# Two MLPs behind a hashed attention: who converts the late weights, and how many conversion steps stand between the second layer's banks

## The chip, the cores and the metric

The kernel runs on one core of one Trainium2 chip. The metric is device time in microseconds (us) of one execution. TensorE (PE) multiplies matrices; its weight loads (PEld) run beside the products. VectorE (DVE), ScalarE (ACT) and GpSimd (POOL) work on tiles, and SyncE (SP) issues DMAs. Each engine takes its instructions in the order in which they were written, and waits on semaphores for the others.

## The reference

Attention with a hash mask, then two MLPs on the same 1536 tokens of width 512. The change lies in the first MLP and in what it prepares for the second.

```
x = attention(q, k, v, proj)                   # 1536 x 512
g = x @ w_gate; val = x @ w_val                # 512 -> 1536
y = (g * sigmoid(g) * val) @ w_out             # 1536 -> 512
h = y @ w_in                                   # 512 -> 1024
solu = h * softmax(h); ln = normalised(solu) * g_ln
out = ln @ w_out2                              # 1024 -> 512
```

The weights are float64 in memory. Every product is made of three, high by high, high by low and low by high, of float32r parts, so every weight is turned from float64 to float32 on the chip and then split into a high part and a low part (the rest).

## The kernel before, in words

**Groups.** The hidden width 1536 is 12 slices of 128, taken in six groups t = 0 to 5 of two slices. The tokens are three blocks of 512. For each group come six *units* (two slices by three blocks, function `hidden`, L1103): a unit is 24 products of 128x512, twelve for the gate and then twelve for the value, in two PSUM banks, and there are two banks of each kind. ScalarE applies Silu to the gate bank into `sg` (L1110), VectorE multiplies it by the value bank (L1111), ScalarE rounds the result to `ah` (L1113), VectorE takes the rest `al` (L1116). Then comes the *second layer* of the group (`summed`, L1127 to L1129): for each of the three blocks four banks `y` of six products each, twelve banks in all. Four PSUM banks serve them, so bank k + 4 cannot begin before bank k has been read. In group 0 ScalarE copies each bank to `yf` (L1137), in the later groups VectorE adds it to `yf` (L1139).

**Conversions.** Beside this runs a generator `stream` of 25 *pieces* of weights, each a 1 MB DMA into a buffer `raw` (two of them, L944 to L952), and conversion in *steps*, each of which is one call of `go(stream)`. `to_float32` is six VectorE instructions (L47, L51, L53, L57, L62, L64) from `raw` to the one buffer `wf`; L64 stands in a step with the ScalarE copy that follows it. Then ScalarE takes the high part (L1039) and VectorE the low part (L958). A piece of kind 1 (first layer) or 2 (second layer) is seven steps. The *late* pieces are for the second MLP: kind 3 are four row blocks of `w_in`, from which sums of blocks are made as well (`blocks3`; GpSimd makes t2, t3 and t4 at L989 to L1002), and kind 4 are four pairs of row blocks of `w_out2`, scaled by `g_ln`, split in place in `raw` and stored to DRAM (`parked`, L1025). Pieces 3/0 and 3/2 are last in group 0, 3/1 in group 1, 3/3 in group 2, 4/0 in group 3, 4/2 in group 4, 4/4 and 4/6 in group 5. The buffer `raw` of piece n is fetched again, for piece n + 2, when piece n has done with it.

**Order.** The order on every engine is that of the Python code (`manual_schedule`). A unit takes one step behind its products and up to three more, ending at the step "copied". In the second layer steps stand ahead of the reading of each bank: in group 0 two per bank (24 over three blocks), in groups 1 to 4 one, two, one, two (18 over three blocks). A step that comes when the next piece may not yet begin (`reached`) does nothing.

Of the kernel before, what the change touches and what calls it, by code (L numbers as in the profile page):

```python
# [9 lines left out]
F32 = mybir.dt.float32  # L10
# [6 lines left out]
ALU = mybir.AluOpType  # L17
# [11 lines left out]
def run(steps):  # L29
    for _ in steps:  # L30
        pass
# [6 lines left out]
def to_float32(nc, raw, f):  # L38

    words = raw.bitcast(I32).rearrange("p (n t) -> p n t", t=2)
    low, high = words[:, :, 0], words[:, :, 1]
    bits = f.bitcast(I32)


    nc.vector.tensor_scalar(  # L47
        bits, high, 1, 1, ALU.logical_shift_left, ALU.logical_shift_right
    )
    yield  # L50
    nc.vector.tensor_scalar_max(f, f, FLOOR)  # L51
    yield
    nc.vector.tensor_scalar(  # L53
        bits, bits, 3, 0x3FFFFFF8, ALU.logical_shift_left, ALU.bitwise_and
    )
    yield
    nc.vector.scalar_tensor_tensor(  # L57
        bits, high, -0x40000000, bits, ALU.bitwise_and, ALU.bitwise_or
    )
    yield  # L60

    nc.vector.tensor_scalar_mul(high, low.bitcast(U32), 2.0 ** -29)  # L62
    yield
    nc.vector.tensor_tensor(bits, bits, high, ALU.add)  # L64
# [3 lines left out]
def hash_attention_then_two_mlps(  # L68
# [16 lines left out]
    nc = tc.nc  # L85
# [12 lines left out]
    BLK = 512  # L98
# [68 lines left out]
    for g in range(4):  # L167
        m = (g + 1) % 2
# [8 lines left out]
    up, down, both = slice(0, D), slice(D, P), slice(0, P)  # L177
# [41 lines left out]
    with at:  # L219
# [13 lines left out]
        one = sm.tile([P, 1], F32, tag="one", name="one", bufs=1)  # L233
# [4 lines left out]
        raw, turned, bits_of, last_of = {}, {}, {}, {}  # L238
# [475 lines left out]
        def go(work):  # L714

            next(work, None)
# [157 lines left out]
    gl = sm2.tile([P, KF2], F32, name="gl", bufs=1)  # L874
# [16 lines left out]
    def halves(pool):  # L891
        return [
            pool.tile([P, 2, DM], R32, tag=tag, name=tag) for tag in ("hi1", "lo1")
        ]
# [4 lines left out]
    with ExitStack() as m1:  # L899
# [16 lines left out]
        def weights1(f):  # L916
            hi, lo = halves(ws)
            w1_of[f] = [x.rearrange("p n (k f) -> p n k f", k=KD) for x in (hi, lo)]
            return hi, lo

        hi, lo = weights1(0)
# [35 lines left out]
        def low(dst, src, hi):  # L957
            nc.vector.tensor_sub(dst, src, hi.bitcast(F32))  # L958

        def blocks3(n, wf):  # L960

            i, d = divmod(n, KH)
            left, right, other = wf[:, :BLK], wf[:, BLK:], w1f[d]
            b11, b21, b22, t1, t2, t3, t4 = (
                [w3_of[x][:, m, d] for m in range(2)]
                for x in ("b11", "b21", "b22", "t1", "t2", "t3", "t4")
            )
            if i == 0:  # L970
                nc.scalar.copy(b11[0], left)
                nc.scalar.copy(other, right)
                yield "copied"
                low(b11[1], left, b11[0])
                nc.vector.tensor_sub(left, right, left)
                nc.scalar.copy(t1[0], left)
                yield "copied"
                low(t1[1], left, t1[0])
                return
            nc.scalar.copy(b21[0], left)  # L980
            nc.scalar.copy(b22[0], right)  # L981
            yield "copied"
            low(b21[1], left, b21[0])
            low(b22[1], right, b22[0])
            add, sub = nc.gpsimd.tensor_add, nc.gpsimd.tensor_sub
            for block, first, t in ((b22, sub, t3), (b11, add, t2), (b21, sub, t4)):
                hi, lo = (x.bitcast(F32) for x in block)
                if first is sub:
                    sub(other, hi, other)  # L989
                else:  # L990
                    add(other, other, hi)
                add(other, other, lo)
                rounded(*t, other)

        def rounded(hi, lo, src):

            n = src.shape[1:]
            one = unit1
            for _ in n[1:]:
                one = one.unsqueeze(2)  # L1000
            nc.gpsimd.tensor_mul(hi, src, one.to_broadcast(list(src.shape)))
            nc.gpsimd.tensor_sub(lo, src, hi.bitcast(F32))  # L1002

        def convert(piece, raw):
            kind, n = piece[2:4]
            wf = wr.tile([P, 2 * DM], F32, tag="wf", name="wf", bufs=1)
            yield from to_float32(nc, raw, wf)
            if kind == "4":

                hi, lo = (  # L1010
                    raw.bitcast(R32)[:, m * 2 * DM:(m + 1) * 2 * DM].rearrange(
                        "p (m e) -> p m e", m=2
                    ) for m in range(2)
                )
                wf = wf.rearrange("p (m e) -> p m e", m=2)
                for m in range(2):
                    nc.scalar.mul(hi[:, m], wf[:, m], gl[:, n + m:n + m + 1])
                yield "copied"
                for m in range(2):
                    nc.vector.scalar_tensor_tensor(  # L1020
                        lo[:, m], wf[:, m], gl[:, n + m:n + m + 1], hi[:, m].bitcast(F32),
                        ALU.mult, ALU.subtract,
                    )
                for m, x in enumerate((hi, lo)):
                    nc.sync.dma_start(parked[m][n // 4][:, n % 4:n % 4 + 2], x.bitcast(F32))  # L1025
                return
            if kind == "3":
                yield from blocks3(n, wf)
                return
            if kind == "1":  # L1030
                hi, lo = weights1(n)
            else:
                hi, lo = [
                    w2.tile([P, 2, DM], R32, tag=f"{x}2", name=f"{x}2") for x in ("hi", "lo")
                ]
                for m in range(2):
                    w2_of[n + m] = [x[:, m] for x in (hi, lo)]
            hi, lo = (x.rearrange("p m e -> p (m e)") for x in (hi, lo))
            nc.scalar.copy(hi, wf)  # L1039
            yield "copied"  # L1040
            low(lo, wf, hi)

        def conversions():

            raws = [fetch(piece) for piece in pieces[:AHEAD]]
            for n, piece in enumerate(pieces):
                while piece[:2] > reached:
                    yield
                yield from convert(piece, raws[n])
                if n + AHEAD < len(pieces):  # L1050
                    raws.append(fetch(pieces[n + AHEAD]))
                yield
# [100 lines left out]
        stream = conversions()  # L1153
# [3 lines left out]
        for t in range(TH):  # L1157
            for unit in range((FT + 1) * NBLK):
                f, blk = divmod(unit, NBLK)
                reached = (t, unit)  # L1160
                if t == TH - 1 and unit == FT * NBLK:

                    yh = xpool.tile([P, KD, NT], R32, tag="h", name="yh")
                    yl = xpool.tile([P, KD, NT], R32, tag="l", name="yl")
                    run(stream)
                    for n in (0, 2):
                        parts = halves(ws)
                        for x, stored in zip(parts, parked):
                            nc.sync.dma_start(x.bitcast(F32), stored[0][:, n:n + 2])
                        for m in range(2):  # L1170
                            w4_of[n + m] = [x[:, m] for x in parts]
                    nc.scalar.activation(half, half, AF.Exp)
                work = hidden(t * FT + f, blk) if f < FT else summed(t, blk)
                go(work)
                if f < FT:

                    go(stream)
                    go(before)
                    for _ in range(3):
                        if next(stream, None) == "copied":  # L1180
                            break
                    go(work)
                    before = work
                    continue

                go(before)
                before = lows(blk - 1) if t == TH - 1 and blk else iter(())
                for d in range(KD):
                    if blk and t == TH - 1:
                        go(before)  # L1190
                    else:
                        go(stream)
                        if t == 0 or d % 2:
                            go(stream)
                    go(work)
        sums_of(1)
# [264 lines left out]
```

## Time and profile before

| | |
|---|---|
| median of three runs | 718.27 us (717.79 to 718.29) |
| the profiled execution | 717.94 us, its span 716.2 us |
| PE busy | 688.2 us, 96% of the span |
| DVE busy | 588.0 us, 82% |
| ACT busy | 353.4 us, 49% |
| POOL busy | 255.2 us, 36% |
| mean granted TensorE clock | 0.988 of full speed |

The span runs from the first to the last instruction; 1.74 us lie around it. The profile puts each idle time of an engine down to the instruction that ended it. A matmul is pipelined, so its duration is longer than the pitch from start to start, and the pitch is what counts.

### The profile page before, as it was taken

How to read it: one execution, taken by the hardware profiler on the slowest of the kernel's cores; microseconds unless marked ns; L12 is line 12 of the kernel's file. 1: busy time of each engine (PE TensorE's matmuls, PEld its weight loads, DVE VectorE, ACT ScalarE, POOL GpSimd, SP SyncE). 2: the span in 40 equal slices, each digit the busy share in tenths (PEclk: the TensorE clock that was granted, in tenths of full speed). 3: DMA queues.
4: the chain of work that ended last, by engine and by line, in shares of the span. 5: the costliest groups of instructions: out<-in, count | busy, mean ns of one | idle time of the engine just before them, and what ended most of it. 6: DMA issues, size and time to landing. Idle time of an engine off the chain costs nothing.

```text
span 716.2 us, 10379 instructions
## 1 busy us (share of the span) xinstructions
PE 688.2 (96%) x3653; PEld 585.4 (82%) x3653; DVE 588.0 (82%) x1046; ACT 353.4 (49%) x724; POOL 255.2 (36%) x271
## 2 busy tenths in 40 slices
PE   8999999999999999879989889999999999999998
PEld 6999999999998888658768668778778887888877
DVE  8989999999999988897866896785887887756771
ACT  7898898988989742324122112213113534424332
POOL 6656556655534510370000370000000177775300
PEclk9999999999999999989999999999999999999999
DMA  5684563654514122313122111331333530222211
GB/s 176 168 206 119 157 164 86 159 153 104 145 44 146 18 88 91 117 59 117 59 72 95 69 59 59 118 118 60 118 117 119 176 118 1 88 89 89 89 45 45
DMA packets 39492, 73.72 MB, mean 103 GB/s; under 512 B 5352, under 2 KB 26920, under 8 KB 38672
## 3 DMA queue, kind: packets, MB, share of 16 engines
q1 hardware_dynamic: 39440, 73.06, 33.4%
q8 instruction: 29, 0.48, 0.3%
q14 instruction: 23, 0.19, 0.1%
HBM read 40.90 MB, written 7.34 MB: 67 GB/s over the span
## 4 chain that ended last, share of the span: by engine, by line
PE 72%; DVE 21%; ACT 4%; issue 2%; DMA 1%; SPq 0%; DVEq 0%; ACTq 0%
PE h L1103 21%; PE s L539 9%; PE t L589 8%; PE h L1216 7%; PE av L624 4%; PE av L628 3%; PE o L1331 3%; PE o L1329 3%; PE o L1330 3%; DVE wf L57 2%; DVE wf L64 2%; PE pp L498 2%; DVE yf L1139 2%; PE pp L455 2%; DVE raw L62 1%
## 5 line engine op out<-in xcount | busy, mean ns | idle before, releaser
L1103 PE MATMUL h<-xh,hi 128*128 128x512 f32 x288 | 113.9, 396 | 4.5 <-DVE sg L1111 4.5
L1103 PE MATMUL h<-xl,hi 128*128 128x512 f32 x288 | 113.5, 394 | 0.0
L1103 PE MATMUL h<-xh,lo 128*128 128x512 f32 x288 | 112.5, 394 | 0.0
L602 DVE TENSOR_TENSOR el<-t,eh 128x384 fp32r<-128x384 f32 x192 | 97.7, 550 | 9.7 <-ACT eh L598 8.7
L574 ACT ACTIVATE e<-s,nm 128x768 f32<-128x768 f32 x96 | 97.7, 1017 | 4.6 <-DVE nm L559 4.0
L598 ACT CAST eh<-t 128x384 fp32r<-128x384 f32 x192 | 83.9, 492 | 18.5 <-PE t L589 16.8
L550 DVE TENSOR_REDUCE top<-s 128x1 f32<-128x768 f32 x96 | 90.6, 944 | 0.7 <-PE s L539 0.5
L589 PE MATMUL t<-idr,e 128*128 128x128 f32 x576 | 80.1, 274 | 0.5 <-DVE el L602 0.3
L589 PEld LDWEIGHTS t<-idr,e 128*128 128x128 f32 x576 | 67.9, 140 | 9.4 <-DVE el L602 3.9
L1127 PE MATMUL y<-ah,hi 128*128 128x512 f32 x144 | 59.7, 415 | 15.2 <-DVE yf L1139 13.2
L1103 PEld LDWEIGHTS h<-xh,hi 128*128 128x128 f32 x288 | 55.1, 191 | 16.5 <-DVE sg L1111 4.9
L1111 DVE TENSOR_TENSOR sg<-h,sg 128x512 f32<-128x512 f32 x36 | 24.9, 691 | 48.5 <-PE h L1103 39.7
L1103 PEld LDWEIGHTS h<-xl,hi 128*128 128x128 f32 x288 | 55.0, 191 | 11.4
L1103 PEld LDWEIGHTS h<-xh,lo 128*128 128x128 f32 x288 | 54.8, 191 | 11.5
L624 PE MATMUL av<-eh,vs 128*128 128x384 f32 x186 | 64.0, 344 | 0.0
L1113 ACT CAST ah<-sg 128x512 fp32r<-128x512 f32 x36 | 22.4, 623 | 81.4 <-DVE sg L1111 81.4
L1129 PE MATMUL y<-ah,lo 128*128 128x512 f32 x144 | 57.8, 402 | 0.0
L1128 PE MATMUL y<-al,hi 128*128 128x512 f32 x144 | 57.8, 401 | 0.0
L539 PE MATMUL s<-ka,qa 128*128 128x384 f32 x192 | 54.6, 365 | 1.5 <-ACT e L574 1.4
L1066 POOL TENSOR_TENSOR sf<-yh 128x256 f32<-128x256 f32 x5 | 3.7, 736 | 142.1 <-ACT yh L1142 142.1
L1039 ACT CAST hi<-wf 128x1024 fp32r<-128x1024 f32 x17 | 17.8, 1048 | 72.6 <-DVE wf L64 72.6
L989 POOL TENSOR_TENSOR w1f<-w3b,w1f 128x512 f32<-128x512 f32 x4 | 7.0, 1760 | 129.7 <-ACT w3b L981 129.5
(274 smaller groups left out, 1609.0 us busy)
## 6 DMA issues: line engine op xcount, KB each, us to landing
raw<-in_moe_w_out_dram SPq DMA_DIRECT2D x10, 1024.0 KB
raw<-in_moe_w_gate_dram SPq DMA_DIRECT2D x12, 512.0 KB
raw<-in_moe_w_val_dram SPq DMA_DIRECT2D x12, 512.0 KB
ka<-kt SPq DMA_DIRECT2D x30, 192.0 KB
moved<-u SPq DMA_DIRECT2D x9, 512.0 KB
raw<-in_moe_w_in_dram SPq DMA_DIRECT2D x4, 1024.0 KB
parked<-raw SPq DMA_DIRECT2D x8, 512.0 KB
v<-in_v_dram SPq DMA_DIRECT2D x8, 384.0 KB
```

The source lines that it names most:

```text
L539: nc.tensor.matmul(s[:, n, :HALF], a[:, rows], m[:, n * HALF:(n + 1) * HALF], start=first, stop=not first,)
L550: nc.vector.tensor_reduce(top[:, 1:2], s_of[i][:, :, :HALF], AX.XY, ALU.max, negate=True)
L574: nc.scalar.activation(e, s_of.pop(i)[:, :, :HALF], AF.Exp, bias=nm[:, 1:2], scale=nm[:, 0:1], accum_out=total_of[p, n][:, j, c:c + 1],)
L589: nc.tensor.transpose(t[:, m, :], e_of[i][:, g, m * P:(m + 1) * P], idf)
L598: nc.scalar.copy(half_tile(eh_of, i, g), t_of[i, g])
L602: last_of[i] = nc.vector.tensor_sub(half_tile(el_of, i, g), t_of.pop((i, g)), half_tile(eh_of, i, g).bitcast(F32),)
L624: nc.tensor.matmul(av, vj[:, c], eh_of[h][:, c, :], start=c == 0, stop=c == C - 1)
L1103: nc.tensor.matmul(ps[n], a[:, n, kk, :], x[:, kk, blk * BLK:(blk + 1) * BLK], start=kk == 0 and a is hi and x is xh, stop=kk == KD - 1 an ...
L1127: nc.tensor.matmul(p, hi[:, cols], ah, start=f == t * FT, stop=False)
L1128: nc.tensor.matmul(p, hi[:, cols], al, start=False, stop=False)
L1129: nc.tensor.matmul(p, lo[:, cols], ah, start=False, stop=f == (t + 1) * FT - 1)
L1216: nc.tensor.matmul(dst, a[m](d), w3_of[b][:, l, d], start=start and n == 0, stop=n == 3 * KH - 1, skip_group_check=True,)
```

## The change

Late pieces: of kind 3 with i = 0 (3/0 and 3/1), VectorE keeps the low part of b11; the difference for t1 and its split go to GpSimd, in `raw` as scratch. With i = 1 (3/2, 3/3) the low part of b22 goes to GpSimd. In kind 4 ScalarE writes the scaled weights where the low part will stand, then copies the high part, and GpSimd subtracts. So no step holds more than one VectorE instruction. In the second layer three steps stand to four banks (one, none, one, one) in groups 1 to 4, and five (one, two, one, one) in group 0.

```diff
@@ blocks3
-        def blocks3(n, wf):
+        def blocks3(n, wf, raw):
...
+            add, sub = nc.gpsimd.tensor_add, nc.gpsimd.tensor_sub
             if i == 0:
                 nc.scalar.copy(b11[0], left)
                 nc.scalar.copy(other, right)
                 yield "copied"
                 low(b11[1], left, b11[0])
-                nc.vector.tensor_sub(left, right, left)
-                nc.scalar.copy(t1[0], left)
-                yield "copied"
-                low(t1[1], left, t1[0])
+                one = raw.bitcast(F32)[:, :BLK]
+                sub(one, other, b11[0].bitcast(F32))
+                sub(one, one, b11[1].bitcast(F32))
+                rounded(*t1, one)
                 return
...
             low(b21[1], left, b21[0])
-            low(b22[1], right, b22[0])
-            add, sub = nc.gpsimd.tensor_add, nc.gpsimd.tensor_sub
+            sub(b22[1], right, b22[0].bitcast(F32))
@@ convert, kind 4
+                both = lo.bitcast(F32)
                 for m in range(2):
-                    nc.scalar.mul(hi[:, m], wf[:, m], gl[:, n + m:n + m + 1])
+                    nc.scalar.mul(both[:, m], wf[:, m], gl[:, n + m:n + m + 1])
                 yield "copied"
-                for m in range(2):
-                    nc.vector.scalar_tensor_tensor(
-                        lo[:, m], wf[:, m], gl[:, n + m:n + m + 1], hi[:, m].bitcast(F32),
-                        ALU.mult, ALU.subtract,
-                    )
+                nc.scalar.copy(hi, both)
+                nc.gpsimd.tensor_sub(lo, both, hi.bitcast(F32))
@@ the second layer's banks
-                        go(stream)
-                        if t == 0 or d % 2:
+                        if t == 0 or d != 1:
+                            go(stream)
+                        if t == 0 and d == 1:
                             go(stream)
                     go(work)
```

**VectorE, second layer of group 3, before** (`yf` is a bank's addition; the other rows are conversions, L1020 the low part of piece 4/0):

```order
L57 SCALAR_TENSOR_TENSOR wf<-raw,wf 128x1024
L1139 TENSOR_TENSOR yf<-y,yf 128x512
L62 TENSOR_SCALAR raw<-raw 128x1024
L64 ISA wf<-raw,wf 128x2048
L1139 TENSOR_TENSOR yf<-y,yf 128x512
L1020 SCALAR_TENSOR_TENSOR raw<-wf,gl,raw 128x512 x2
L1139 TENSOR_TENSOR yf<-y,yf 128x512
L47 TENSOR_SCALAR wf<-raw 128x1024
L51 TENSOR_SCALAR wf<-wf 128x1024
L1139 TENSOR_TENSOR yf<-y,yf 128x512
L53 TENSOR_SCALAR wf<-wf 128x1024
L1139 TENSOR_TENSOR yf<-y,yf 128x512
```

The same place now (the addition is L1137 in the changed file):

```order
L57 SCALAR_TENSOR_TENSOR wf<-raw,wf 128x1024
L1137 TENSOR_TENSOR yf<-y,yf 128x512 x2
L62 TENSOR_SCALAR raw<-raw 128x1024
L1137 TENSOR_TENSOR yf<-y,yf 128x512
L64 ISA wf<-raw,wf 128x2048
L1137 TENSOR_TENSOR yf<-y,yf 128x512 x3
L47 TENSOR_SCALAR wf<-raw 128x1024
L1137 TENSOR_TENSOR yf<-y,yf 128x512
L51 TENSOR_SCALAR wf<-wf 128x1024
L1137 TENSOR_TENSOR yf<-y,yf 128x512
```

Five additions had eight conversions between and ahead of them; now eight additions have five.

**VectorE, from the second `w_in` piece of group 0 to the first `sg` of group 1, before** (`lo` is a kind 1 weight's low part, `sg` the product of the first unit):

```order
L47 TENSOR_SCALAR wf<-raw 128x1024
L51 TENSOR_SCALAR wf<-wf 128x1024
L53 TENSOR_SCALAR wf<-wf 128x1024
L57 SCALAR_TENSOR_TENSOR wf<-raw,wf 128x1024
L62 TENSOR_SCALAR raw<-raw 128x1024
L64 ISA wf<-raw,wf 128x2048
L958 TENSOR_TENSOR lo_4379<-wf,hi_4378 128x1024
L47 TENSOR_SCALAR wf<-raw 128x1024
L51 TENSOR_SCALAR wf<-wf 128x1024
L53 TENSOR_SCALAR wf<-wf 128x1024
L57 SCALAR_TENSOR_TENSOR wf<-raw,wf 128x1024
L1111 TENSOR_TENSOR sg<-h_4390,sg 128x512
```

The same place now:

```order
L47 TENSOR_SCALAR wf<-raw 128x1024
L51 TENSOR_SCALAR wf<-wf 128x1024
L53 TENSOR_SCALAR wf<-wf 128x1024
L57 SCALAR_TENSOR_TENSOR wf<-raw,wf 128x1024
L62 TENSOR_SCALAR raw<-raw 128x1024
L64 ISA wf<-raw,wf 128x2048
L1109 TENSOR_TENSOR sg<-h_4382,sg 128x512
L958 TENSOR_TENSOR lo_4410<-wf,hi_4409 128x1024
```

The first `sg` moves ahead of five conversions, which follow it.

**ScalarE, second layer of group 0, before** (`yf` are the banks' copies, `w3b` and `w3t` parts of the late pieces):

```order
L1137 COPY yf<-y 128x512
L971 CAST w3b_3963<-wf 128x512
L972 COPY w1f_96<-wf 128x512
L976 CAST w3t_3966<-wf 128x512
L1137 COPY yf<-y 128x512 x4
L980 CAST w3b_3964<-wf 128x512
L981 CAST w3b_3965<-wf 128x512
L1137 COPY yf<-y 128x512 x3
L1039 CAST hi_4378<-wf 128x1024
L1137 COPY yf<-y 128x512 x4
L1110 ACTIVATE sg<-h_4389 128x512
```

The same place now:

```order
L1135 COPY yf<-y 128x512
L972 CAST w3b_3963<-wf 128x512
L973 COPY w1f_96<-wf 128x512
L1135 COPY yf<-y 128x512 x6
L981 CAST w3b_3964<-wf 128x512
L982 CAST w3b_3965<-wf 128x512
L1135 COPY yf<-y 128x512 x5
L1037 CAST hi_4409<-wf 128x1024
L1108 ACTIVATE sg<-h_4381 128x512
```

The `w3t` copy is gone, the second piece's two copies stand behind the seventh bank and not the fifth, and the last five banks come ahead of the kind 1 copy.

## Rows read from the trace of the kernel before

**Rows 1.** Longest waits of PE, 280 to 590 us: total, times, longest.

```profile
PE y L1127 <- DVE yf L1139: 13.2, 15, 2.3
PE h L1103 <- DVE sg L1111: 4.5, 1, 4.5
PE y L1127 <- ACT yf L1137: 1.8, 1, 1.8
```

**Rows 2.** Windows: stretch, length, busy PE, PEld, DVE, ACT, POOL, PEclk, DMA, GB/s.

```profile
281.96:341.85 59.89, 53.63 (x218) 42.99 (x216) 50.69 (x51) 18.90 (x32) 19.71 (x12) 0.91 0.26 88
341.85:397.42 55.57, 51.85 (x217) 41.44 (x216) 40.59 (x54) 12.02 (x18) 0.00 (x0) 0.97 0.23 76
397.42:454.80 57.38, 52.01 (x218) 41.07 (x217) 45.88 (x53) 11.41 (x17) 19.05 (x12) 0.97 0.22 74
454.80:507.47 52.67, 50.53 (x218) 40.19 (x216) 39.89 (x53) 11.60 (x17) 0.00 (x0) 1.00 0.29 100
507.47:560.13 52.66, 50.53 (x217) 40.19 (x216) 42.96 (x57) 12.12 (x19) 0.00 (x0) 1.00 0.28 100
```

**Rows 3.** The chain in order of time, six units of group 4: start, us, what.

```profile
474.97 32.67 PE h L1103 x144
```

**Rows 4.** Timeline of PE, groups 0 and 1: start, us, instruction, [idle before, releaser].

```profile
290.72 0.57 PE L1127 MATMUL y<-ah,hi 128*128 128x512 f32 x1 [1.80 <-ACT yf L1137]
302.26 0.39 PE L1103 MATMUL h<-xh,hi 128*128 128x512 f32 x1
320.52 0.80 PE L1103 MATMUL h<-xh,hi 128*128 128x512 f32 x1 [4.46 <-DVE sg L1111]
```

**Rows 5.** Windows behind two PE waits, columns as above; PEclk is third from the end.

```profile
290.90:294.20 3.30, 3.30 (x9) 2.54 (x10) 3.16 (x5) 1.22 (x3) 0.00 (x0) 0.52 0.29 101
318.20:324.90 6.70, 4.38 (x10) 3.48 (x11) 5.01 (x6) 2.16 (x3) 0.58 (x1) 0.51 0.09 20
```

**Rows 6.** Timeline of DVE, second layer of group 3, GpSimd idle.

```profile
457.05 1.22 DVE L57 SCALAR_TENSOR_TENSOR wf<-raw,wf 128x1024 int32<-128x1024 int32 x1
458.19 0.68 DVE L1139 TENSOR_TENSOR yf<-y,yf 128x512 f32<-128x512 f32 x1
458.79 0.69 DVE L62 TENSOR_SCALAR raw<-raw 128x1024 int32<-128x1024 uint32 x1
459.51 1.23 DVE L64 CUSTOM_DVE_ANT_0 wf<-raw,wf 128x2048 uint16<-128x2048 uint16 x1
461.53 1.42 DVE L1020 SCALAR_TENSOR_TENSOR raw<-wf,gl,raw 128x512 fp32r<-128x512 f32 x2 [0.19 <-ACT raw L1017]
```

**Rows 7.** Timeline of DVE beside a busy GpSimd, groups 0 and 2.

```profile
303.34 2.19 DVE L57 SCALAR_TENSOR_TENSOR wf<-raw,wf 128x1024 int32<-128x1024 int32 x1
305.56 1.67 DVE L62 TENSOR_SCALAR raw<-raw 128x1024 int32<-128x1024 uint32 x1
409.79 0.68 DVE L1139 TENSOR_TENSOR yf<-y,yf 128x512 f32<-128x512 f32 x1
```

**Rows 8.** Timeline of POOL, first and last of the twelve instructions of piece 3/3.

```profile
404.61 1.29 POOL L989 TENSOR_TENSOR w1f<-w3b,w1f 128x512 f32<-128x512 f32 x1 [85.83 <-ACT w3b L981]
423.52 1.61 POOL L1002 TENSOR_TENSOR w3t<-w1f,w3t 128x512 fp32r<-128x512 f32 x1
```

**Rows 9.** Timeline of DVE and ACT, group 0: late conversion, bank copies, first `sg` of group 1.

```profile
287.46 0.62 ACT L971 CAST w3b<-wf 128x512 fp32r<-128x512 f32 x1 [3.31 <-DVE wf L64]
290.08 2.04 ACT L1137 COPY yf<-y 128x512 f32<-128x512 f32 x4
309.49 1.05 ACT L1039 CAST hi<-wf 128x1024 fp32r<-128x1024 f32 x1 [10.53 <-DVE wf L64]
319.79 0.68 DVE L1111 TENSOR_TENSOR sg<-h,sg 128x512 f32<-128x512 f32 x1
```

**Rows 10.** Timeline of SP and a window of the DMAs: a weight fetch and its end.

```profile
296.36 0.37 SPq L952 DMA_DIRECT2D raw<-in_moe_w_out_dram  x1
...
300.00:302.00 2.00, 2.00 (x10) 1.69 (x9) 1.93 (x3) 0.00 (x0) 1.92 (x2) 1.00 0.29 119
```

More of the change, by code (lines that the diff above doesn't have):

```diff
@@ L1027, in convert @@
             if kind == "3":
-                yield from blocks3(n, wf)
+                yield from blocks3(n, wf, raw)
                 return
```

## Prediction

> **What bounds the kernel now.** I read the waits of PE first, from 280 to 590 us, where the diff works [rows 1]. PE waits there for almost one thing: the additions of the second layer's banks to `yf`, 13.2 us in 15 waits, with 1.8 us for a ScalarE copy and 4.5 us for one late `sg`. Then I cut the stretch at the first product of each second layer, into five stages (0 to 4, one second layer and the next group's six units each), and asked for the busy times of each [rows 2]. They last 59.89, 55.57, 57.38, 52.67 and 52.66 us. The chain of waits gives what a stage needs: 144 products in 32.67 us, 0.227 us each [rows 3]. A stage has 72 + 144 = 216 products, so 49.0 us. The rest is loss: 10.9, 6.6, 8.4, 3.7 and 3.7, together 33.3 us. That is more than the 19.5 us of waits. A stall costs PE part of its overlap besides (groups 3 and 4 lose 3.7 us each), and behind the longer waits the granted clock is 0.51 to 0.52, the 1.2 GHz level, for 3.3 or 6.7 us [rows 5].
>
> VectorE is not full: it is busy 39.9 to 50.7 us of each stage [rows 2]. It is late where the work is bunched. Twelve banks of 6 x 0.227 = 1.36 us come in 16.3 us, and between them stand 18 conversion steps. The bank k + 4 waits for bank k's addition, so the eighth addition is the last one that PE can wait for, and it must be done 11 x 1.36 = 15.0 us into the second layer.
>
> **The change part by part.** I count from a stage's first product. Alone, a conversion instruction comes every 0.69 to 0.73 us (L47, L51, L53, L62) or 1.22 to 1.26 us (L57, L64), an addition every 0.60 [rows 6]. Beside a busy GpSimd the first kind takes 1.67 and the second 2.2, about 1.0 us more each, while an addition stays at 0.68 [rows 7].
>
> *Steps, groups 3 and 4.* L57 starts at 2.25 [457.05 against 454.80, rows 2, 6]. Now: L57 to 3.4, two additions to 4.6, L62 to 5.3, an addition to 5.9, L64 to 7.1, three additions (the sixth bank ends at 8.2) to 9.1, L47 to 9.8, the seventh to 10.4, L51, the eighth. L51 may meet the new GpSimd instruction: ScalarE's scaling ends at about 8.6, its new 128x1024 copy (1.05 as in [rows 9]) at 9.7, and GpSimd then takes, by twice the 1.29 of a 128x512 one, an estimated 2.6 us [rows 8]. If L51 waits for all of it, the eighth addition is done at 13.6. PE wants it at 15.0. No stall; a gain of 3.7 in each. Two VectorE instructions of 0.71 [rows 6] go, and the estimated 2.6 us on GpSimd stands beside PE work.
>
> *Steps, group 1.* GpSimd now has four instructions for 3/1, from 8.3 (L64 ends at 7.1, two ScalarE copies follow) to about 15. L47 and L51 become 1.67. Additions: fourth 7.7, fifth 9.1 behind L958, sixth 9.7, seventh 12.0, eighth 14.3. Slack 0.7; gain 6.6.
>
> *Steps, group 2.* GpSimd runs thirteen instructions instead of twelve, which took 404.61 to 425.13, 1.71 each [rows 8], so from 8.3 to about 30. The eighth addition is done at 14.3 as in group 1. Behind it everything is slow: L53 15.7, two additions, L57 19, L62 and two additions, L64 at about 23, ScalarE's copy 24, L958 26, L47 and L51, then the first `sg` at 29.6. PE wants it when the third unit reaches its value bank, 16.3 + 2.5 x 5.45 = 29.9. The second `sg` comes at 35.5 and is wanted at 35.4. I take 0.5 us of loss: gain 7.9.
>
> *Group 0.* Before: ScalarE's second copy stood behind `w3t`, so PE resumed at 290.72 [rows 4]; at 1.36 us per bank it would have been 288.8. Now that copy comes behind `w1f`, at about 289.1: 0.4 us of loss. But 3/0 now has four GpSimd instructions from 288.6 on, beside the six conversions of 3/2. Alone these would end at 294.2, with 3.6 us for the four about 297.8. The eighth bank's copy now stands behind the two copies that wait for that: done at 299.5, wanted at 297.4. So a new stall of 2.1, and perhaps the low clock behind it. The units start at 300.9 (302.5 with the low clock) against 302.26 [rows 4]. Thirteen GpSimd instructions follow, to 320. L958, the wait for GpSimd to read `wf`, and six conversions at 1.4 to 2.2 us put L64 at 310.3; ScalarE's copy and Silu to 312.0, first `sg` to 312.7. It was wanted two and a half units after the start: 314.5 or 316. Before, it was done at 320.5 [rows 9] and cost 4.46 us and a low clock [rows 4]. The second `sg` (L958 2.2, `al`, L47, L51, L53 first) is done at 321.1, wanted at 320.0 or 321.6. Two and a half units more end at 334.7 or 335.2. I take 335.0 against 341.85: gain 6.9.
>
> *Costs taken at nothing.* Steps moved into the units of groups 1 to 5: the units there issue the same sequence as before from the second `sg` on (in group 1 from the fifth), and of the 49.0 us VectorE has 9 free in stage 3 and 6 in stage 4 [rows 2]; without that cover a late `sg` costs what stage 0 paid. The buffer `raw` of 3/0 and 3/1 is held until GpSimd has done, some 7.5 us, and with it a fetch on SP's queue. A fetch lands about 4.3 us after its issue (issued at 296.36, the last DMA time about 300.6) [rows 10]: in group 0 at 299.3, wanted at 300.3; in group 1 at 19, wanted at 24. In kind 4 the store waits for GpSimd until about 12.3 instead of 8.2 and holds the next fetch behind it on SP; that lands at about 20, wanted at 24. If one of these fetches is late, VectorE's queue stands, with additions or `sg` behind it; each us would be a us.
>
> Sum: 6.9 + 6.6 + 7.9 + 3.7 + 3.7 = 28.8. From the profiled execution's 717.94 (span 716.2 and 1.74 around it) that leaves 689.1; I say 689. The median before lies 0.33 above that execution. Bounds: all the loss goes, 717.94 - 33.3 = 684.6; or GpSimd makes it worse, below.
>
> What a VectorE instruction loses to GpSimd is 1.0 us here, the rest of the GpSimd instruction in progress [rows 7, 8]. The Trainium skill (SBUF — State Buffer, "SBUF: two separate sides") speaks against giving GpSimd work: the shared port pair is "an exclusive lock, not a bandwidth split", held for the whole instruction, for VectorE instructions that read two SBUF inputs or use both ports. The trace agrees: conversions go from 0.69 to 1.67, the additions, one input of which is PSUM, stay. By that rule the 128x1024 instruction blocks L51 for its whole length, which is the upper case taken above; by 1.0 us the eighth addition would be done at 12.2 and the sum is the same.
>
> **The rivals.** *GpSimd's longer work keeps VectorE late.* If each extra GpSimd instruction costs VectorE all of its 1.65 us and not 1.0, the late conversions of group 0 end 2.6 us later and its first `sg` and second `sg` some 7 us later in all: stage 0 gains nothing. In stage 2 the `sg` come 4 us late: gain 4. Groups 1, 3 and 4 keep 6.6 + 3.7 + 3.7. Sum 18, so 700. For it: group 0 lost 10.9 us beside twelve such instructions. Against: groups 3 and 4, which lost 7.4 with GpSimd idle, are mended by the order alone.
>
> *The waits move from `yf` to `sg` (the other side).* Nine steps per stage leave the second layer and stand in the units. If the first `sg` is late past the third unit's value bank in every stage as it was in group 0, each pays 4.46 of wait [rows 4] and half of 6.7 us at the low clock [rows 5], 7.8. The units of groups 2 to 5 would pay 31.2, against 25.5 that go (33.3 less the 7.8 that the units of group 1 pay already): 717.9 + 31.2 - 25.5 = 724. It decides where the first `sg` comes more than 13.6 us after the units' start. My count has it 5 us early in groups 1, 3 and 4 (at 24 to 25 against 29.9), so this needs conversions a third slower than any row.
>
> *The waits change their name only*, since PE is held by something else that ends at the same time: 717 to 719. Against it, the profile names nothing else within PE's waits [rows 1].
>
> **How the numbers follow.** Forecast 0.62, its own range 685 to 694. GpSimd keeps VectorE late, 694 to 705: 0.28. Waits move to `sg`, slower: 0.05. No change: 0.03. What is left, 0.02, is faster in some other way. About 0.2% (1.4 us) is what a measurement of this kernel can tell from no change. So faster 0.92, same 0.03, slower 0.05. The range 685 to 701 holds the forecast and two thirds of the second case.
>
> **What would show it.** Right: no wait of PE for `yf` above a few tenths of a us; stages 1, 3 and 4 at 49.0 to 49.5; stage 0 at about 53, with a wait for a ScalarE `yf` copy near 297 to 299; stage 2 at 49 to 50; low clock in at most one or two stretches, in stage 0. Wrong: waits for `sg` in the third or fourth unit of groups 1 and 3 above 2 us; VectorE waiting for a DMA into `raw`, which it never does now; the eighth addition still late behind L51 in group 2; a lower clock in stretches without waits.

## The result, and the profile after

The changed kernel takes 700.44 us (median of four runs, 700.32 to 701.35), against 718.03 for the kernel before. The ratio is 0.976, with a 95% interval of 0.974 to 0.978. That is 17.6 us less. The forecast was 28.8 us less, so the direction and the range held, and 11 us of the gain did not come. The profiled execution's span is 698.7 us.

The stages, cut as in [rows 2], with the second layer of group 5 added (start and end, length, busy PE, PEld, DVE, ACT, POOL, granted clock, DMA share, GB/s):

```profile
282.21:338.61 56.40, 50.45 (x218) 40.15 (x216) 47.59 (x44) 17.25 (x30) 26.87 (x17) 1.00 0.24 80
338.61:391.38 52.77, 50.86 (x217) 41.59 (x216) 43.26 (x57) 12.30 (x19) 5.99 (x4) 0.97 0.28 94
391.38:443.26 51.88, 49.25 (x217) 40.46 (x216) 45.73 (x52) 11.12 (x17) 21.00 (x13) 1.00 0.25 81
443.26:492.22 48.96, 48.96 (x217) 40.54 (x216) 39.85 (x51) 12.45 (x18) 2.40 (x1) 1.00 0.30 108
492.22:541.18 48.96, 48.96 (x217) 40.54 (x216) 41.97 (x52) 12.99 (x19) 4.96 (x2) 1.00 0.29 108
541.18:558.56 17.38, 16.61 (x73) 13.44 (x72) 14.72 (x23) 10.97 (x18) 9.13 (x8) 1.00 0.52 180
```

Stages 3 and 4 are at the floor: PE is busy for the whole 48.96 us. Stages 0, 1 and 2 lose 7.4, 3.8 and 2.9 us over that floor, and the last second layer loses 1.1 (its floor is 16.32, what its 72 products take at their pitch). PE's waits from 270 to 590 us, which answer to [rows 1]:

```profile
PE h L1101 <- ACT sg L1108: 5.8, 3, 2.6
PE y L1125 <- DVE yf L1137: 2.7, 2, 1.9
PE y L1125 <- ACT yf L1135: 2.2, 2, 2.0
PE o L1330 <- DVE ll L1316: 0.7, 2, 0.5
PE h L1101 <- DVE sg L1109: 0.6, 1, 0.6
```

The waits for the additions fell from 13.2 us to 2.7. A new one leads: three waits for `sg` as ScalarE's Silu writes it (L1108), which PE did not have before. The longest stands in group 3's units. VectorE, ScalarE and PE there, in order of time:

```profile
423.96 1.23 DVE L64 CUSTOM_DVE_ANT_0 wf<-raw,wf 128x2048 uint16<-128x2048 uint16 x1
...
425.22 1.04 ACT L1037 CAST hi<-wf 128x1024 fp32r<-128x1024 f32 x1 [5.05 <-DVE wf L64]
426.17 0.59 ACT L1108 ACTIVATE sg<-h 128x512 f32<-128x512 f32 x1
...
426.79 0.69 DVE L1109 TENSOR_TENSOR sg<-h,sg 128x512 f32<-128x512 f32 x1 [1.61 <-ACT sg L1108]
...
426.81 0.50 PE L1101 MATMUL h<-xh,hi 128*128 128x512 f32 x1 [2.63 <-ACT sg L1108]
```

This is the Silu of the second unit. Its gate bank has long been full: PE began that unit's value bank at 415.86. Silu stands in ScalarE's queue behind the 1024-wide high copy of a weight piece, and that copy waits for L64 on VectorE, which is late. When Silu is done, PE gets the bank back, for the gate products of the fourth unit.

The same lateness comes out in group 1's second layer. The stage begins at 338.61; the prediction had L57 start 2.25 us later. It starts 5.64 us later:

```profile
344.25 1.22 DVE L57 SCALAR_TENSOR_TENSOR wf<-raw,wf 128x1024 int32<-128x1024 int32 x1
345.38 1.28 DVE L1137 TENSOR_TENSOR yf<-y,yf 128x512 f32<-128x512 f32 x2
...
346.12 0.50 PE L1125 MATMUL y<-ah,hi 128*128 128x512 f32 x1 [1.91 <-DVE yf L1137]
```

The stretch that begins 1.3 us behind that product, in the columns of the stages:

```profile
347.40:350.70 3.30, 3.30 (x9) 2.56 (x8) 3.22 (x5) 1.14 (x2) 0.45 (x1) 0.51 0.00 0
```

PE waits 1.91 us for the first addition, and then the clock is at the 1.2 GHz level for 3.3 us, which is worth 1.6 us. Together that is nearly all of the stage's 3.8. In group 5 one of the new GpSimd instructions shows what it does to a conversion:

```profile
534.85 2.56 POOL L1021 TENSOR_TENSOR raw<-raw 128x1024 fp32r<-128x1024 f32 x1 [30.58 <-ACT raw L1020]
...
535.18 2.78 DVE L51 TENSOR_SCALAR wf<-wf 128x1024 f32<-128x1024 f32 x1
```

L51, 0.69 us alone, lasts 2.78, and ends 0.55 us behind the GpSimd instruction.

### The profile page after: what moved, and what is told of

The parts are those of the page before. It is cut to its first block, busy times and chain, and to the rows that moved or that the text cites. A ratio compares the mean times of both kernels' runs of the same rounds, so it can differ in the third digit from the quotient of the medians.

```text
span 698.7 us, 10396 instructions
## 1 busy us (share of the span) xinstructions
PE 679.0 (97%) x3653; PEld 583.0 (83%) x3653; DVE 586.5 (84%) x1032; ACT 354.8 (51%) x726; POOL 281.2 (40%) x285
## 5 line engine op out<-in xcount | busy, mean ns | idle before, releaser
L1101 PE MATMUL h<-xh,hi 128*128 128x512 f32 x288 | 112.5, 391 | 6.4 <-ACT sg L1108 5.8
L1101 PE MATMUL h<-xl,hi 128*128 128x512 f32 x288 | 112.1, 389 | 0.0
L1125 PE MATMUL y<-ah,hi 128*128 128x512 f32 x144 | 57.2, 397 | 4.9 <-DVE yf L1137 2.7
L1021 POOL TENSOR_TENSOR raw<-raw 128x1024 fp32r<-128x1024 f32 x4 | 9.8, 2441 | 118.4 <-ACT raw L1020 71.8
L628 PE MATMUL av<-el,vs 128*64 128x384 f32 x155 | 52.2, 337 | 0.0
```

Of the source, the lines that this page charges most:

```text
L628: nc.tensor.matmul(*low, start=False, stop=False)
L1101: nc.tensor.matmul(ps[n], a[:, n, kk, :], x[:, kk, blk * BLK:(blk + 1) * BLK], start=kk == 0 and a is hi and x is xh, stop=kk == KD - 1 an ...
L1125: nc.tensor.matmul(p, hi[:, cols], ah, start=f == t * FT, stop=False)
```

## The experiments

Each kernel was timed beside the kernel before. PE's loss over its floor is given by stage, from each profile (48.96 us for stages 0 to 4, 16.32 for the second layer of group 5). The attention ahead of stage 0 ends up to 2.45 us earlier or later from one profiled execution to the next (281.96 to 284.41), so causes are read from the stages.

| kernel | median us | ratio to before, 95% | stage 0 | 1 | 2 | 3 | 4 | last |
|---|---|---|---|---|---|---|---|---|
| before | 718.0 | | 10.9 | 6.6 | 8.4 | 3.7 | 3.7 | 0 |
| changed | 700.44 | 0.974 to 0.978 | 7.4 | 3.8 | 2.9 | 0 | 0 | 1.1 |
| steps only | 696.91 | 0.969 to 0.972 | 5.4 | 3.8 | 2.5 | 0 | 0 | 0 |
| offload only | 719.25 | 1.001 to 1.003 | 12.2 | 5.1 | 8.7 | 4.0 | 4.0 | 0 |
| changed, Silu first | 692.23 | 0.963 to 0.966 | 4.9 | 2.5 | 0 | 0 | 0 | 0 |
| changed, t1 back | 699.51 | 0.973 to 0.977 | 5.9 | 3.8 | 2.9 | 0 | 0 | 1.1 |
| changed, kind 4 back | 698.94 | 0.971 to 0.976 | 9.1 | 0.6 | 2.9 | 0 | 0 | 0 |
| steps, Silu first | 690.99 | 0.960 to 0.964 | 2.8 | 4.1 | 0 | 0 | 0 | 0 |
| the same, sums later, two per unit | 696.88 | 0.969 to 0.972 | 0.7 | 2.9 | 0.3 | 7.0 | 0 | 0 |
| steps, sums later, Silu behind | 704.08 | 0.978 to 0.982 | 0.8 | 5.6 | 4.3 | 7.2 | 0 | 0 |
| steps, Silu first, one sum per unit, groups 2 to 5 | 687.92 | 0.956 to 0.959 | 0.7 | 0 | 0 | 0 | 0 | 1.3 |
| the same, first five units of groups 1 to 5 | 685.48 | 0.954 to 0.956 | 0.7 | 0 | 0 | 0 | 0 | 0 |

**Fewer steps alone.** The kernel before with the second layer's steps of the change:

```diff
-                        go(stream)
-                        if t == 0 or d % 2:
+                        if t == 0 or d != 1:
+                            go(stream)
+                        if t == 0 and d == 1:
                             go(stream)
```

> The kernel before with the second layer's fewer steps alone; the late pieces stay on VectorE as they were. Theory (the order gives the gain, the work given to GpSimd costs about as much as it spares): 698 to 703 us, groups 3 and 4 lose under 1 us each (before 3.7), GpSimd idle in the second layer of group 1. Rival (the gain needs the VectorE instructions taken away): 706 to 712, with waits for the additions left in groups 3 and 4.

Measured 696.91, 1.1 us under the theory's range and 3.5 us better than the whole change. Stages 3 and 4 are at the floor, so the order alone mends them. The loss of the last second layer is gone, and so is PE's 2.0 us wait for a ScalarE copy in group 0. The waits for Silu stay, so they need no work on GpSimd beyond the sums that it made before:

```profile
PE h L1103 <- ACT sg L1110: 5.4, 3, 2.2
PE y L1127 <- DVE yf L1139: 1.9, 1, 1.9
PE h L1103 <- DVE sg L1111: 0.5, 1, 0.5
PE y L1127 <- ACT yf L1137: 0.2, 1, 0.2
```

**The offload alone.** The changed kernel with the steps of before.

> The changed kernel with the steps of before (two per bank in group 0, six to four banks later); the late pieces are split over GpSimd and ScalarE. Theory (order gives the gain): 712 to 720 us, PE waits for the additions stay near 10 us or more. Rival (offload gives it): 703 to 708.

Measured 719.25, no gain and by its interval 0.1 to 0.3% slower than before. Waits of PE:

```profile
PE y L1125 <- DVE yf L1137: 15.1, 13, 2.9
PE y L1125 <- ACT yf L1135: 6.3, 2, 6.0
PE h L1101 <- ACT sg L1108: 1.1, 1, 1.1
PE h L1101 <- DVE sg L1109: 1.0, 1, 1.0
```

One VectorE instruction less here and there does not pay for the GpSimd instruction that stands beside the next conversions. With this and the run above the parts are told apart: the steps gave 21.1 us, and the offload took 3.5 of them back, 2.0 in stage 0, 0.5 in stage 2 and 1.1 at the end.

**Silu ahead of the steps.** The changed kernel, ScalarE's order alone:

```diff
             nc.scalar.activation(sg, ps[0], AF.Silu)
+            yield
             nc.vector.tensor_mul(sg, ps[1], sg)
...
                     go(stream)
+                    go(work)
                     go(before)
```

> The changed kernel with a unit's Silu issued on ScalarE ahead of the stream's steps, so that it no longer stands behind the 1024-wide high copy that waits for VectorE's L64. VectorE's order is untouched. Theory (what the change left, 11 us short of the forecast, is this queue on ScalarE: L64, high copy, Silu, sg, one after the other): the three waits for Silu of 5.8 us go and the late units' tail into the second layer of groups 1 and 5 with them; 690 to 694 us. Rival (GpSimd holds VectorE, so sg is late however ScalarE is ordered): 698 to 700, the waits are put down to VectorE's sg instead.

Measured 692.23, 8.2 us better than the change, as the theory had it. No wait for `sg` above 0.15 us is left, and with the waits went the loss in stage 2 and at the end:

```profile
PE y L1126 <- ACT yf L1136: 2.2, 2, 2.0
PE y L1126 <- DVE yf L1138: 2.2, 1, 2.2
```

The rival, that the waits would only change their name to VectorE's `sg`, is out. In stages 0 and 1 7.4 us stay.

**t1 back on VectorE.** The changed kernel, with the lines of before for pieces 3/0 and 3/1:

```diff
-                one = raw.bitcast(F32)[:, :BLK]
-                sub(one, other, b11[0].bitcast(F32))
-                sub(one, one, b11[1].bitcast(F32))
-                rounded(*t1, one)
+                nc.vector.tensor_sub(left, right, left)
+                nc.scalar.copy(t1[0], left)
+                yield "copied"
+                low(t1[1], left, t1[0])
```

> The changed kernel with the difference and split for t1 (pieces 3/0 and 3/1) back on VectorE with its ScalarE copy, the rest as changed. Theory of GpSimd's hold: the conversions of 3/2 in group 0 end some 2 us earlier, the 2.0 us wait for a ScalarE bank copy goes, stage 0 is 2 to 3 us shorter: 697 to 699 us. Theory of ScalarE's queue alone: 699.5 to 701, since the late Silu sets stage 0's end anyway.

Measured 699.51, with runs from 698.89 to 701.19, so the total decides nothing. Stage 0 does: 54.86 instead of 56.40, and the 2.0 us wait for a ScalarE copy is gone, as the theory of GpSimd's hold says. Of the 2.0 us, 0.5 come back as a longer wait for Silu, so the stage is 1.5 us shorter and not 2 to 3.

**Kind 4 back on VectorE.** The changed kernel, with the lines of before for kind 4 (two `scalar_tensor_tensor` on VectorE in place of the ScalarE copy and the GpSimd subtraction).

> The changed kernel with the low part of the kind 4 pieces back on VectorE. Theory (one 128x1024 GpSimd instruction of 2.56 us held VectorE's L51 for 2.78 us in the last group and made its last sg late): the second layer of group 5 is back at 16.3 us from 17.4, the other stages stay: about 699.4 us. Rival (the last group's loss is ScalarE's extra copy or the store behind it): no change in stage 5 unless that copy goes too, so this run cannot show the rival alone; 700.4.

Measured 698.94. The last second layer is at its floor again, so the offload of kind 4 cost 1.1 us there and gained nothing in stages 3 and 4. The ScalarE copy went with the GpSimd instruction, so this run does not part the two; the last `sg` of group 5 starts 1.62 us into the second layer here and 3.65 in the change, and the 2.0 us between are about what L51 lost to GpSimd. With Silu first both stay, L51 lasts 2.77 us, and the last second layer is at its floor all the same: the hold costs PE time there only with Silu behind the copies. Stages 0 and 1 are not touched by the edit, and yet differ, 9.1 and 0.6 us against 7.4 and 3.8: the clock fell in stage 0 in this execution and in stage 1 in that of the change, and a PE that is held earlier may give VectorE time to catch up. The two are read together, 9.7 against 11.2, and the 1.5 us between them stay unexplained.

**Fewer steps and Silu first,** without the offload.

> The kernel before with the fewer steps and with Silu ahead of the stream's steps; no late work on GpSimd or ScalarE beyond before. If the two effects add (offload costs 3.5, Silu's place 8): 688 to 690 us, stage 0 at 51 to 52, stage 1 at 50 to 52, the rest at 49.0. If what Silu's place gave was the same time that the offload took: 692 to 694.

Measured 690.99, and 690.07 to 691.92: between the two outcomes, a little above the first. The effects add only in part. Against the change with Silu first, stage 0 loses 2.0 us less, as with Silu behind, but stage 1 loses 1.6 more, so 7.0 us of loss are left in the two: a 1.8 us wait for VectorE's `sg` and a 2.2 us wait for an addition, with a low clock.

**The GpSimd sums later, two per unit.** The same, with the twelve GpSimd instructions of 3/2 and of 3/3, which are as old as the kernel before, taken out of the second layers and issued in pairs from the fourth unit of group 1 on, each behind that unit's `sg`:

```diff
+                    if (t, f) > (1, 0):
+                        sums_later(2)
```

> As the run with fewer steps and Silu first, and the GpSimd sums of pieces 3/2 and 3/3 (twelve instructions each) issued two per unit from the fourth unit of group 1 on, each behind that unit's sg. Theory (what is left in stages 0 and 1 is VectorE held by these twelve): stages 0 and 1 fall to 49 to 50, all loss but 1 us is gone: 685 to 687 us. Rival (VectorE has too much to do there in any case): 688 to 690, no better than without this.

Measured 696.88: worse, and outside both ranges. Stage 0, where GpSimd now works for 7.0 us, all in the last units, instead of 19.7, is at 49.71, as the theory said. Stage 1 still loses 2.9, and stage 3, which had no loss, loses 7.0. The pairs in the units ahead of it (GpSimd is busy for 14.3 us of stage 2) make VectorE late: L57 comes 6.71 us into stage 3, where it came 2.26 in without them, and the last pair stretches the last unit's `al` and L57 besides. PE waits 4.05 us, and the granted clock is 0.94 over the stage. GpSimd, VectorE and PE there:

```profile
440.39 1.59 POOL L1009 TENSOR_TENSOR w3t<-w1f,w3t 128x512 fp32r<-128x512 f32 x1
...
440.78 2.28 DVE L57 SCALAR_TENSOR_TENSOR wf<-raw,wf 128x1024 int32<-128x1024 int32 x1
442.98 1.28 DVE L1156 TENSOR_TENSOR yf<-y,yf 128x512 f32<-128x512 f32 x2
...
443.71 0.80 PE L1144 MATMUL y<-ah,hi 128*128 128x512 f32 x1 [4.05 <-DVE yf L1156]
```

**The same with Silu behind the high copy.**

> As the run with the fewer steps alone, with the GpSimd sums spread behind later units, but Silu where it was, behind the high copy. Theory of GpSimd's hold as the root (VectorE in time, so L64 and the high copy are done before Silu is due): Silu's place costs nothing and this equals the run with both, 685 to 688 us. Theory of ScalarE's queue as a cause of its own: waits for Silu of some us stay, 690 to 694.

Measured 704.08, over both ranges, since the pairs themselves cost time, as in the run above; the two runs are compared stage by stage. Stage 0 is 49.72, the same as with Silu first (49.71): where VectorE is in time, Silu's place costs nothing. In stages 1 and 2, where the pairs make VectorE late, it costs 2.8 and 4.1 us, of which some 1.6 each are the low clock behind the wait (granted clock 0.97 over these stages, 1.00 in the run above). No wait of PE is put down to Silu here: VectorE's `sg` waits for it (1.61 us at 330.45), and PE waits for the additions behind, 11.4 us in three waits against 6.4 in two. So ScalarE's queue is not a cause by itself. It passes VectorE's lateness on to PE.

**One sum per unit,** with fewer steps and Silu first, in groups 2 to 5, or in the first five units of groups 1 to 5:

```diff
+                    if t > 1:
+                        sums_later(1)
```

```diff
+                    if t and unit < FT * NBLK - 1:
+                        sums_later(1)
```

> Fewer steps, Silu first, the 24 GpSimd sums of pieces 3/2 and 3/3 one per unit in groups 2 to 5, so that none runs in stage 0 and in the units of group 1. Theory (the wait for the additions in the second layer of group 1 is VectorE's lateness carried over from GpSimd's hold in the stage before): stages 0 and 1 are both 49 to 50 and no stage loses over 1 us: 685 to 687 us. Rival (that wait is the conversions themselves, too many for the units of group 1): stage 1 stays at 51 to 53, 688 to 691.

> The same with one sum per unit in the first five units of groups 1 to 5, none behind the last unit of a group, where the additions follow. If one instruction per unit is within VectorE's spare time (9 us of 49): as the run before, 685 to 688 us. If the units of group 1 have none to spare: stage 1 loses 2 to 3 us, 688 to 690.

Measured 687.92 and 685.48. In both, stage 1 is at 48.96: the wait in group 1's second layer was lateness carried over from GpSimd's hold in the stage before. In the first, a sum beside the last unit of group 5 makes the additions late, and PE waits 1.0 us in the last second layer. In the second, nothing is left but 0.7 us in stage 0, where a ScalarE copy of a bank is 0.2 us late. Its first two stages:

```profile
282.15:331.85 49.70, 49.48 (x218) 40.38 (x216) 44.02 (x50) 19.44 (x32) 8.81 (x5) 1.00 0.31 106
331.85:380.81 48.96, 48.96 (x218) 40.54 (x216) 44.54 (x54) 11.93 (x18) 8.74 (x5) 1.00 0.25 87
```

This version beats both kernels: 0.955 of before (0.954 to 0.956). VectorE is busy for 44 us of 49, with GpSimd beside it for 8.8, and PE waits for it nowhere from stage 0 to the last second layer.

## Why the prediction was right, and where it was not

**Steps in groups 3 and 4: right.** 3.7 and 3.7 us were forecast, and 3.71 and 3.70 came (52.67 and 52.66 to 48.96 each). The run with fewer steps alone shows that the order did it. The reading behind it, that the loss of a stage is its length less 216 products at their pitch and not the sum of the waits, is borne out: 7.4 us came back where 4.1 us of waits stood.

**The offload, costed at nothing there: right for these two stages only.** The 128x1024 instruction took 2.4 to 2.6 us as estimated. L51 was held to its end, the upper case that the prediction took: it lasted 2.22 and 2.27 us in groups 3 and 4, and in group 3 the eighth addition was done at 13.2, forecast at 13.6 and wanted at 15.0. (For a hold of 1.0 us the prediction gives 12.2; by its own prices that is 12.7, which changes nothing.) The Trainium skill (SBUF — State Buffer, "SBUF: two separate sides") has the two engines lock each other out of a port that they share; the 2.78 us of L51 agree with it. The prediction let this time stand beside PE work. In group 5 that cover was gone: L51's 2.1 us made the last `sg`, `al` and additions late, which cost 1.1 us at the end that the sum did not have.

**Group 0: the first half right, the term mis-sized.** The new wait for a ScalarE copy was forecast as 2.1 us near 297 to 299 and measured as 1.99 at 299.83; L64 was forecast to end at 310.3, and ended at 311.8; the second `sg` at 321.1, and 322.4. What followed on ScalarE and PE, by time:

```profile
309.58 2.20 DVE L64 CUSTOM_DVE_ANT_0 wf<-raw,wf 128x2048 uint16<-128x2048 uint16 x1
311.81 1.05 ACT L1037 CAST hi<-wf 128x1024 fp32r<-128x1024 f32 x1 [9.70 <-DVE wf L64]
312.76 0.59 ACT L1108 ACTIVATE sg<-h 128x512 f32<-128x512 f32 x1
313.40 0.50 PE L1101 MATMUL h<-xh,hi 128*128 128x512 f32 x1 [1.02 <-ACT sg L1108]
322.42 0.50 PE L1101 MATMUL h<-xh,hi 128*128 128x512 f32 x1 [0.56 <-DVE sg L1109]
327.59 0.50 PE L1101 MATMUL h<-xh,hi 128*128 128x512 f32 x1 [2.16 <-ACT sg L1108]
```

The first of these waits shows what the count left out. It gave `sg` a deadline at the value bank, two and a half units behind the start. But the gate bank is freed by Silu alone, and PE wants it half a unit (2.7 us) earlier, at the start of the third unit: the first `sg` was in time, and the Silu ahead of it was not. Then the walk stopped at the second `sg`, with "two and a half units more". The third Silu stands behind the next L64 and high copy, and cost 2.16 us at the start of the fifth unit. The gain was 3.5, not 6.9.

**Group 1: the term failed at its start.** The 6.6 us rested on L57 at 2.25 us, the place of before in group 3 [rows 6]. VectorE was still late from group 0, so that L57 came at 5.64, and at 5.60 in the run with fewer steps alone: the GpSimd work of before is enough for it. The gain was 2.8. The slack of 0.7 us found for the eighth addition was never the question: the first one was late.

**Group 2: mis-sized, by the wrong deadline.** 7.9 forecast, 5.5 came. The count puts L64 at about 23 where its own prices add up to 24.2; it was done at 20.8, so the slip did no harm. The first `sg` was in time, as counted, and the second was counted to 35.5 us and done at 36.1. The prediction compared it with the fourth unit's value bank, wanted at 35.4, and took 0.5 us of loss. But the Silu just ahead of it frees the gate bank, which the fourth unit wants at 16.3 + 3 x 5.45 = 32.7. By the prediction's own count that Silu ends at about 34.8, which would have given some 2 us of loss; PE waited 2.63.

**The step that failed,** in the prediction's words, is that the units "issue the same sequence as before" and so hide the moved steps. The sequence is the same, but it comes on top of a VectorE that is late, by 3.4 us at L57 in group 1, and ScalarE's order, in which a Silu follows a copy that waits for VectorE, turns that into waits of PE. The prediction asked when each `sg` frees a value bank, and never when each Silu frees a gate bank, which PE wants 2.7 us earlier. The differences are 3.4, 3.8, 2.4 and 1.1 us in these four places, and 0.7 outside the stages, which is the 11.4 by which the profiled executions (717.94 and 700.51) differ from the sum.

**What the range owes to luck.** The forecast's own range, 685 to 694, was missed. The stated range, to 701, held the result by 0.6 us, and only because it took in part of the first rival's case. Of the signs named for being wrong one came, a wait for `sg` above 2 us in the fourth unit of group 3, and of those for being right several did not: PE still waits 1.91 us for `yf`, and stages 0, 1 and 2 are at 56.4, 52.8 and 51.9, not at 53, 49 and 49 to 50.

**The rivals.** The first, GpSimd keeping VectorE late, had the time (700) and the engine, but not the way. It put the cost down to the extra GpSimd instructions, and the run without them shows that these cost 3.5 us of the 11; most of the rest comes with the sums that GpSimd made before. It also had the wrong distribution: it gave stage 0 no gain and stage 1 all of its 6.6, and stage 0 gained 3.5 while stage 1 gained 2.8. The second, waits that move from `yf` to `sg`, was seen too, though as 6.4 us and not 31: its place, the units, was right, but it looked at VectorE's `sg`, and what PE waited for was mostly Silu (5.8 of the 6.4). What the runs show together: GpSimd's hold makes L64 late, and ScalarE's queue hands it on. Take the offload away, or Silu's place, and part comes back (3.5 and 8.2 us); take both away and spread the sums, and all but 0.7 us does.

## What to carry to other kernels

Price a move to another engine by what it does to the instructions that will run beside it, not by the engine's idle share: GpSimd was busy for only 36% of the span before the change, and the work given to it, alone, gained nothing (719.25 us against 718.04). When an order is changed, walk every queue to the end of the stage, and ask of each short instruction that PE waits for (here Silu) whether it stands behind one that waits for a late engine. Give each buffer the deadline of the instruction that frees it: here the gate bank, freed by Silu, was wanted 2.7 us ahead of the value bank, freed by `sg`. Take the loss of a stage from its length against its products, since a wait costs more than its idle time.

## What the runs showed of the hardware

Additions with a PSUM operand kept their 0.60 us pitch beside GpSimd. In the kernel before, four of them and two GpSimd instructions:

```profile
418.63 2.31 POOL L989 TENSOR_TENSOR w1f<-w3b,w1f 128x512 f32<-128x512 f32 x1
419.72 2.48 DVE L1139 TENSOR_TENSOR yf<-y,yf 128x512 f32<-128x512 f32 x4
421.02 1.30 POOL L992 TENSOR_TENSOR w1f<-w1f,w3b 128x512 f32<-128x512 f32 x1
```

Conversions in SBUF grew by nearly what was left of the GpSimd instruction in progress when they began: L51 in group 5 by 2.09 us, with 2.23 left.

The granted clock did not follow the wait alone. Behind the same wait of 1.99 us for a ScalarE copy it stayed at full speed in the profile of the change, and was at the 1.2 GHz level for most of 3.4 us in that of the change with Silu first. Both stretches begin 2.0 us behind the product that ended the wait:

```profile
301.85:305.25 3.40, 3.40 (x17) 2.80 (x16) 3.33 (x3) 0.26 (x1) 3.17 (x4) 1.00 0.15 61
```

```profile
303.00:306.40 3.40, 3.40 (x11) 2.67 (x10) 3.33 (x3) 0.28 (x1) 3.17 (x4) 0.58 0.19 77
```

That is 1.4 us between two executions with the same wait, more than some of the edits here are worth, and a reason to read the stages and not one total.
